# Four tiles' loads and transposes ahead of the weight pieces, and the second product of four tiles in step with w2

## The chip, the cores and the metric

The kernel runs on one core of a Trainium2 chip. The time is the device time of one execution in microseconds (us); a median of several runs is given, and beside it one execution taken with a profiler.

## The reference

The kernel computes banded attention with a per-head distance bias, followed by a normalised two-layer network with a residual. There are 4 batches, 8 heads, 768 tokens and a head size of 64; the model width is 512 and the inner width 2048. The weights arrive as 8-byte floats.

```
keep   = (col < n_global) | (0 <= row - col < n_local)       # 8 and 96
scores = q @ k.T / 8 - slope[h] * dist ; scores[~keep] = -1e9
a      = softmax(scores)
x      = (a @ v), heads side by side                          # [4, 768, 512]
xn     = (x - mean) / sqrt(var + 1e-6) * g_ln
out    = x + relu(xn @ w_ch1) @ w_ch2                         # [512,2048], [2048,512]
```

## The kernel before

**Tiles.** The 3072 tokens are cut into 24 tiles of 128 (`TILES`): first the four tiles at the head of each batch, which see only themselves (tiles 0 to 3, one key block), then the other twenty, which see their own block and the one before (two key blocks). Two tiles are a chunk (`CT = 2`), and the network works on a chunk of 256 tokens.

**A tile's way.** `keys` loads k, splits each value into two halves of 16 bits (`kn`, high and low part) and transposes them by DMA into `kT`; `attention` does the same with q (`qn`, `qT`, plus two DMAs, line 199, that lay a copy with the halves exchanged), and `values` with v, without a transpose. Then come the scores on TensorE (line 225), the mask and minimum on VectorE (230), the exponential on ScalarE (234), the split of the result (237 or 239, and 240 on GpSimd), a transposing DMA `pT<-pn` (242) and the product with v (250 to 252). `norm` ends the tile: statistics, scaling, a split, and a transposing DMA `xT<-xn` (273). A chunk's network waits for `xT` of both its tiles. All DMAs are issued from one queue, SyncE's (SP).

**The network.** `ffn1(c, f)` computes two blocks of 128 inner units for chunk c: 24 matmuls of 256 columns (lines 316 to 318), a ReLU (320) and a split (321) into a tile `h` of the pool `hpool` (17 buffers of 2 KB a partition). A chunk has eight such groups. `ffn2(c, n_)` computes the second product for one tile: 48 matmuls of 512 columns (331 to 333) into one bank of PSUM, then the residual (337) and the store (339).

**The weights.** They come in 16 pieces of 1 MB, eight of w1 (`weights1(j, c)`) and eight of w2 (`weights2(f)`). A piece is loaded into one of three buffers `st` (line 139), and then takes three passes on ScalarE (142, 144, 147) and three on VectorE (143, 145, 148) to become two matrices of 16-bit floats. Two pieces of w1 serve two groups of `ffn1`; a piece of w2 serves two of the sixteen steps of `ffn2`.

**The order.** The program is traced in Python; a scheduler then fixes each engine's order, in which what was traced earlier goes first among what its own model takes to be ready. Each engine and SP's queue then work in that fixed order. `ORDER` adds constraints: `mk` names instructions, and an entry such as `"D1_0_1": "q0"` puts the load of that piece behind tile 0's q transpose on SP's queue, if that was traced before. The start is traced so:

```
one = tokens(0); four steps of it; build_masks()
weights1(0, 0); weights1(0, 1)
go(both(one, tokens(1)))          # tiles 0 and 1
go(f1w(0, range(NK)))             # w1's other pieces, ffn1 of chunk 0 between them
go(tokens(2)); go(tokens(3))      # tiles 2 and 3
build_mask1(); four pieces of w2; ffn1 of chunk 1, w2's other pieces between
run(ffn2 of tiles 0 to 3, side(tiles 4 to 6), RATE)
```

After that `run` takes each chunk in turn, with the attention of later tiles between its steps (`side`). PSUM has four pools of two banks: `ps_s`, `ps_v`, `ps_1` (first product) and `ps_2` (second product).

## Time and profile before

| | us |
|---|---|
| median of 3 runs | 696.86 |
| lowest and highest | 696.26, 701.62 |
| profiled execution, its own time | 697.23 |
| its span | 695.5 |
| mean granted clock of TensorE | 0.982 of full speed |
| PE busy | 590.6 |
| VectorE (DVE) busy | 391.3 |
| ScalarE (ACT) busy | 293.6 |
| GpSimd (POOL) busy | 153.0 |

The span is the time from the profile's first instruction to its last; 1.7 us of the execution's own time lie outside it. Busy times are sums over the span, and the engines work beside each other. PE is TensorE's matmuls. [...]

### The profile page before, as it was taken

The numbers are of one execution on the slowest core, as the hardware profiler recorded it, in microseconds if no ns is written. First come the engines' busy times: TensorE is split into PE (matmuls) and PEld (weight loads), VectorE is DVE, ScalarE is ACT, GpSimd is POOL, SyncE is SP. The second block draws the span as 40 slices with busy tenths as digits, with TensorE's granted clock in tenths as the row PEclk, the third lists the DMA queues.
The fourth block names the chain that finished last, engine by engine and source line by source line (L and its number), as shares of the span: only waits on it lengthen the run. The fifth ranks groups of instructions, "written<-read, shape, count | busy, mean of one in ns | idle before, by whom it ended". The sixth has DMA issues, their size and how long they took to land. (4 is left out here: it accounts for less than half of the span.)

```text
span 695.5 us, 13443 instructions
## 1 busy us (share of the span) xinstructions
PE 590.6 (85%) x5218; PEld 417.0 (60%) x5218; DVE 391.3 (56%) x976; ACT 293.6 (42%) x752; POOL 153.0 (22%) x141
## 2 busy tenths in 40 slices
PE   1011499999589989989999999799989999999995
PEld 0011376785367577577596596396576586684762
DVE  4889899643657687466366456365445456342111
ACT  4977888423424342344354254253243254140110
POOL 0111213302312312222231322222231232120000
PEclk9999999999789999999999999999999999999998
DMA  9999999717867676766848646866853855231001
GB/s 212 245 295 281 243 290 207 161 21 126 167 113 152 127 153 107 149 124 138 158 96 150 146 97 133 148 108 122 167 116 69 152 89 92 66 62 31 16 1 36
DMA packets 264728, 93.25 MB, mean 134 GB/s; under 512 B 254416, under 2 KB 254416, under 8 KB 264656
## 3 DMA queue, kind: packets, MB, share of 16 engines
q1 hardware_dynamic: 264656, 92.31, 64.6%
q8 instruction: 43, 0.70, 0.4%
q14 instruction: 29, 0.24, 0.1%
HBM read 37.23 MB, written 6.29 MB: 63 GB/s over the span
## 5 line engine op out<-in xcount | busy, mean ns | idle before, releaser
L316 PE MATMUL f<-xT,w1h 128*128 128x256 f16 x768 | 212.1, 276 | 12.6 <-DMA xT<-xn 7.6
L317 PE MATMUL f<-xT,w1h 128*128 128x256 f16 x768 | 212.2, 276 | 0.0
L318 PE MATMUL f<-xT,w1l 128*128 128x256 f16 x768 | 212.1, 276 | 0.0
L240 POOL TENSOR_TENSOR pn<-T,pn 128x512 f16<-128x512 f32 x88 | 105.8, 1203 | 207.9 <-DVE pn L239 103.8
L331 PE MATMUL f<-w2h,h 128*128 128x512 f16 x384 | 146.3, 381 | 0.0
L332 PE MATMUL f<-w2l,h 128*128 128x512 f16 x384 | 146.2, 381 | 0.0
L333 PE MATMUL f<-w2h,h 128*128 128x512 f16 x384 | 145.7, 380 | 0.0
L320 ACT ACTIVATE h<-f 128x512 f16<-128x512 f32 x96 | 56.6, 592 | 128.6 <-PE f L318 128.5
L321 DVE SCALAR_TENSOR_TENSOR h<-f,h 128x512 f16<-128x512 f32 x96 | 65.7, 685 | 69.7 <-ACT h L320 69.5
L225 PE MATMUL s<-kT,qT 128*128 128x128 f16 x704 | 57.1, 230 | 51.4 <-DMA qT<-qn 25.3
L234 ACT ACTIVATE T<-T,mn 128x256 f32<-128x256 f32 (+1 forms) x192 | 92.3, 482 | 3.8
L317 PEld LDWEIGHTS <-w1h 128*128 128x128 f16 x768 | 76.0, 99 | 25.0 <-issue 13.7
L225 PEld LDWEIGHTS <-qT 128*128 128x128 f16 x704 | 48.3, 103 | 61.9 <-DMA qT<-qn 33.8
L316 PEld LDWEIGHTS <-w1h 128*128 128x128 f16 x768 | 76.2, 99 | 11.1 <-issue 0.2
L318 PEld LDWEIGHTS <-w1l 128*128 128x128 f16 x768 | 76.2, 99 | 9.5
L230 DVE CUSTOM_DVE_ANT_0 T<-s,mask 128x256 f32<-128x256 f32 (+1 forms) x192 | 67.2, 396 | 24.3 <-PE s L225 24.0
L250 PE MATMUL pv<-vn,pT 128*128 128x64 f16 x352 | 40.9, 196 | 33.3 <-DMA pT<-pn 33.2
L239 DVE CAST pn<-T 128x512 f16<-128x512 f32 x80 | 40.3, 504 | 46.5 <-ACT T L234 41.7
L333 PEld LDWEIGHTS <-h 128*128 128x128 f16 x384 | 37.8, 98 | 42.1 <-issue 0.8
L332 PEld LDWEIGHTS <-h 128*128 128x128 f16 x384 | 37.7, 98 | 39.4 <-issue 0.5
L331 PEld LDWEIGHTS <-h 128*128 128x128 f16 x384 | 37.7, 98 | 37.7 <-issue 0.6
L250 PEld LDWEIGHTS <-pT 128*128 128x128 f16 x352 | 32.7, 99 | 40.7 <-DMA pT<-pn 37.5
(91 smaller groups left out, 646.5 us busy)
## 6 DMA issues: line engine op xcount, KB each, us to landing
st<-in_moe_w_ch_dram SPq DMA_DIRECT2D x16, 1024.0 KB, 6.2
vf<-in_v_dram SPq DMA_DIRECT2D x27, 256.0 KB, 3.5
kf<-in_k_dram SPq DMA_DIRECT2D x26, 256.0 KB, 3.8
qf<-in_q_dram SPq DMA_DIRECT2D x24, 256.0 KB, 3.3
out_dram<-x SPq DMA_DIRECT2D x24, 256.0 KB, 2.4
qT<-qT SPq DMA_DIRECT2D x46, 128.0 KB, 2.5
pT<-pn SPq DMA_TRANSPOSE x88, 3.2
kT<-kn SPq DMA_TRANSPOSE x27, 3.9
```

The costliest lines, as they stand in the source:

```text
L225: last = chain(last, pe.matmul(ps[:, u, n_ * P:(n_ + 1) * P], lhsT=qT[:, a * H + h, :], rhs=use[n_][0][:, h, :], start=(a == 0), stop=(a = ...
L230: vec.tensor_tensor_reduce(out=T[:, u, :], in0=ps[:, u], in1=mask, scale=1.0 / Z, scalar=3e38, op0=ALU.add, op1=ALU.min, accum_out=nm[:, h ...
L234: mk(f"e{t}_{g}", act.activation(out=T[:, u, :], in_=T[:, u, :], func=AF.Exp, scale=-1.0, bias=mn[:, h:h + 1], accum_out=sm[:, h:h + 1]))
L240: pool.tensor_tensor(out=pn[:, :, 1, :], in0=T, in1=pn[:, :, 0, :], op=ALU.subtract)
L250: last = chain(last, pe.matmul(pv[:, h, :], lhsT=ph, rhs=vv[:, h, :D], start=(n_ == 0), stop=False))
L316: last = chain(last, pe.matmul(ps[:, a], lhsT=w1h[:, kk, fs], rhs=xT[:, kk, :], start=(kk == 0), stop=False))
L317: last = chain(last, pe.matmul(ps[:, a], lhsT=w1h[:, kk, fs], rhs=xT[:, NK + kk, :], start=False, stop=False))
L318: last = chain(last, pe.matmul(ps[:, a], lhsT=w1l[:, kk, fs], rhs=xT[:, kk, :], start=False, stop=(kk == NK - 1)))
L321: mk(f"l{c}_{f}", vec.scalar_tensor_tensor(out=hh[:, 1], in0=ps, scalar=0.0, in1=hh[:, 0], op0=ALU.max, op1=ALU.subtract))
L331: pe.matmul(ps, lhsT=hh[:, 0, tok], rhs=w2h[:, f, :], start=(f == 0), stop=False)
L332: pe.matmul(ps, lhsT=hh[:, 0, tok], rhs=w2l[:, f, :], start=False, stop=False)
L333: pe.matmul(ps, lhsT=hh[:, 1, tok], rhs=w2h[:, f, :], start=False, stop=(f == NF - 1))
```

## The change

Tiles 0 to 3 are traced first, in steps that are dealt out by hand: tile 0's k and q, tile 1's loads, the masks, tile 1's k and q, tile 2's loads, and so on to the loads and the k and q transposes of tile 3. Tiles 0 and 1 are then finished; tiles 2 and 3 run beside `f1w`, in which all eight pieces of w1 now stand (pieces (0,0) and (0,1) too). `ffn1` of chunk 1 follows whole, and after it `ffn2_first`: for each piece of w2, the two steps of the second product that it serves, for all four tiles, into four banks (two of `ps_2`, two of `ps_1`); beside it run tiles 4 to 6.

The loaded and split k, q and v of tiles 1 to 3, `kT` and `vn` of tiles 0 and 1, `qT` of tiles 2 and 3 and the output x of tile 5 lie in buffers of `hpool`. `qT` is two tiles in place of one. The loads of g_ln move behind the loads of tile 0. `ORDER` now holds ten entries beside the sixteen of the line below it. The amount of arithmetic, of weight passes and of transfers is the same.

```
...
 TILES = [(b, 0) for b in reversed(range(B))] + [(b, i) for b in range(B) for i in range(1, NT)]
-ORDER = {"D1_0_1": "q0"}
+ORDER = {"L2": "q0", "L3": "q1", "D1_0_0": "q0", "D1_0_1": "q1", "D1_1_0": "q1", "D1_1_1": "p1_0", "D1_2_0": "q3", "D1_2_1": "p2_0", "L4": "p3_1", "L5": "x3"}
 ORDER.update({f"X{n}": f"l{2 + n // 8}_{2 * n % 16}" for n in range(16)})
...
         if ORDER.get(key) in marks:
             tc.add_manual_dep(ins.ins, marks[ORDER[key]].ins.name, NOSYNC, reason="order")
+    place = {bi: t for t, bi in enumerate(TILES)}
+    def short(b, i, shape, dtype, tag, name, bufs):
+        if 0 < place[b, i] < 2 * CT and not (b, i) in again:
+            return hpool.tile(shape, dtype, tag="h", name=name)
+        return p2.tile(shape, dtype, tag=tag, name=name, bufs=bufs)
+    again = set()
+    def own(b, i, name):
+        if place[b, i] < CT and not (b, i) in again:
+            return hpool.tile([P, H, P], F16, tag="h", name=f"{name}{b}_{i}")
+        return p2.tile([P, H, P], F16, tag=name if i else name + "0", name=f"{name}{b}_{i}", bufs=3 if i else 2)
     def fetch(src, name, b, i):
-        f = p2.tile([P, H, D], F32, tag="ld", name=f"{name}f{b}_{i}", bufs=6)
-        load.dma_start(out=f, in_=src[b, :, i * P:(i + 1) * P, :].rearrange("h p d -> p h d"))
+        f = short(b, i, [P, H, D], F32, "ld", f"{name}f{b}_{i}", 6)
+        mk(f"L{place[b, i]}", load.dma_start(out=f, in_=src[b, :, i * P:(i + 1) * P, :].rearrange("h p d -> p h d")))
         return f
-    early = {name: fetch(src, name, *TILES[0]) for name, src in (("k", k), ("q", q))}
+    early = {}
+    def loads(t, names):
+        for name in names:
+            early[name, t] = fetch({"k": k, "q": q, "v": v}[name], name, *TILES[t])
+    loads(0, "kq")
+    def piece(src, name):
+        st = p3.tile([P, 2, 512], I64, tag="st", name="st" + name, bufs=3)
+        mk("D" + name, load.dma_start(out=st, in_=src))
+        return st
+    def piece1(j, c):
+        return piece(w1[2 * c * P:2 * (c + 1) * P, j * 512:(j + 1) * 512].rearrange("(a p) n -> p a n", a=2), f"1_{j}_{c}")
     cnt = counts(tc, const, load, n_global, n_local)
     ng, nl = cnt[:, 0:1], cnt[:, 1:2]
+    loads(0, "v")
...
     def keys(b, i):
-        kf = early["k"] if (b, i) == TILES[0] else fetch(k, "k", b, i)
-        kn = p2.tile([P, H, P], F16, tag="ld", name=f"kn{b}_{i}", bufs=6)
+        kf = early.pop(("k", place[b, i]), None) or fetch(k, "k", b, i)
+        kn = short(b, i, [P, H, P], F16, "ld", f"kn{b}_{i}", 6)
         act.activation(out=kn[:, :, :D], in_=kf, func=AF.Copy)
         (pool if i else vec).tensor_tensor(out=kn[:, :, D:], in0=kf, in1=kn[:, :, :D], op=ALU.subtract)
-        kT = p2.tile([P, H, P], F16, tag="kT" if i else "kT0", name=f"kT{b}_{i}", bufs=3 if i else 2)
-        sp.dma_start_transpose(out=kT, in_=kn.rearrange("p h d -> p (h d)"))
+        kT = own(b, i, "kT")
+        mk(f"k{place[b, i]}", sp.dma_start_transpose(out=kT, in_=kn.rearrange("p h d -> p (h d)")))
         return kT
     def values(b, i):
-        vf = fetch(v, "v", b, i)
-        vn = p2.tile([P, H, P], F16, tag="vn" if i else "vn0", name=f"vn{b}_{i}", bufs=3 if i else 2)
+        vf = early.pop(("v", place[b, i]), None) or fetch(v, "v", b, i)
+        vn = own(b, i, "vn")
         act.activation(out=vn[:, :, :D], in_=vf, func=AF.Copy, scale=VS)
         vec.scalar_tensor_tensor(out=vn[:, :, D:], in0=vf, scalar=VS, in1=vn[:, :, :D], op0=ALU.mult, op1=ALU.subtract)
         return vn
...
     def attention(t, x, xT, at):
         b, i = TILES[t]
         if i == 1 and b:
+            again.add((b, 0))
             blocks[b, 0] = keys(b, 0), values(b, 0)
             yield
         kT = keys(b, i)
-        qf = early["q"] if t == 0 else fetch(q, "q", b, i)
+        qf = early.pop(("q", t), None) or fetch(q, "q", b, i)
         yield
-        qn = p2.tile([P, H, P], F16, tag="ld", name=f"qn{t}", bufs=6)
+        qn = short(b, i, [P, H, P], F16, "ld", f"qn{t}", 6)
         act.activation(out=qn[:, :, :D], in_=qf, func=AF.Copy, scale=-QS)
         vec.scalar_tensor_tensor(out=qn[:, :, D:], in0=qf, scalar=-QS, in1=qn[:, :, :D], op0=ALU.mult, op1=ALU.subtract)
-        qT = p2.tile([P, 2 * H, P], F16, name="qT")
-        mk(f"q{t}", sp.dma_start_transpose(out=qT[:, :H, :], in_=qn.rearrange("p h d -> p (h d)")))
+        if CT <= t < 2 * CT:
+            qT = [hpool.tile([P, H, P], F16, tag="h", name=f"qT{t}_{a}") for a in range(2)]
+        else:
+            qT = p2.tile([P, 2 * H, P], F16, name="qT")
+            qT = [qT[:, :H, :], qT[:, H:, :]]
+        mk(f"q{t}", sp.dma_start_transpose(out=qT[0], in_=qn.rearrange("p h d -> p (h d)")))
         yield
         for here, there in ((slice(0, D), slice(D, P)), (slice(D, P), slice(0, D))):
             if t == 0:
-                vec.tensor_copy(out=qT[here, H:, :], in_=qT[there, :H, :])
+                vec.tensor_copy(out=qT[1][here], in_=qT[0][there])
             else:
-                load.dma_start(out=qT[here, H:, :], in_=qT[there, :H, :])
+                load.dma_start(out=qT[1][here], in_=qT[0][there])
         yield
         vn = values(b, i)
         blocks[b, i] = kT, vn
...
         c, at = divmod(t, CT)
         if at == 0:
             xTs[c] = p3.tile([P, 2 * NK, CT * P], F16, tag="xT", name=f"xT{c}", bufs=2)
-        xs[t] = xpool.tile([P, H, D], F32, tag="x", name=f"x{t}")
+        xs[t] = hpool.tile([P, H, D], F32, tag="h", name=f"x{t}") if t == 2 * CT + 1 else xpool.tile([P, H, D], F32, tag="x", name=f"x{t}")
         yield from attention(t, xs[t], xTs[c], at)
+    gs = const.tile([P, NK], F32, name="gs")
+    load.dma_start(out=gs, in_=g_ln.rearrange("(c p) -> p c", p=P))
+    gb = const.tile([P, DM], F32, name="gb")
+    load.dma_start(out=gb, in_=g_ln.partition_broadcast(P))
     masks = {}
     def build_masks():
...
         for a in range(2):
             hs[c, f + a] = hh[:, :, a, :]
-    def ffn2(c, n_):
-        t = c * CT + n_
-        tok = slice(n_ * P, (n_ + 1) * P)
-        ps = ps_2.tile([P, DM], F32, tag="f2", name=f"f2_{t}")
-        for f in range(NF):
-            hh = hs[c, f]
-            pe.matmul(ps, lhsT=hh[:, 0, tok], rhs=w2h[:, f, :], start=(f == 0), stop=False)
-            pe.matmul(ps, lhsT=hh[:, 0, tok], rhs=w2l[:, f, :], start=False, stop=False)
-            pe.matmul(ps, lhsT=hh[:, 1, tok], rhs=w2h[:, f, :], start=False, stop=(f == NF - 1))
-            if f % 4 == 3 and f < NF - 1:
-                yield
+    def product2(ps, t, f):
+        c, at = divmod(t, CT)
+        tok = slice(at * P, (at + 1) * P)
+        hh = hs[c, f]
+        return [pe.matmul(ps, lhsT=hh[:, a, tok], rhs=w, start=(f == 0 and n_ == 0), stop=(f == NF - 1 and n_ == 2))
+                for n_, (a, w) in enumerate(((0, w2h[:, f, :]), (0, w2l[:, f, :]), (1, w2h[:, f, :])))]
+    def result(ps, t):
         xx = xs[t].rearrange("p h d -> p (h d)")
         vec.scalar_tensor_tensor(out=xx, in0=ps, scalar=1.0 / (HS * WS), in1=xx, op0=ALU.mult, op1=ALU.add)
         b, i = TILES[t]
         load.dma_start(out=out[b, i * P:(i + 1) * P, :], in_=xx)
+    def ffn2(c, n_):
+        t = c * CT + n_
+        ps = ps_2.tile([P, DM], F32, tag="f2", name=f"f2_{t}")
+        for f in range(NF):
+            product2(ps, t, f)
+            if f % 4 == 3 and f < NF - 1:
+                yield
+        result(ps, t)
+        yield
+    def ffn2_first():
+        ps = [ps_2.tile([P, DM], F32, tag="f2", name=f"f2_{t}") if t < 2 else ps_1.tile([P, DM], F32, tag="f1", name=f"f2_{t}") for t in range(2 * CT)]
+        for f in range(0, NF, 2):
+            weights2(f // 2)
+            for t in range(2 * CT):
+                product2(ps[t], t, f)
+                product2(ps[t], t, f + 1)
+                yield
+        for t in range(2 * CT):
+            result(ps[t], t)
         yield
     def ffn(c):
...
     def f1w(c, js):
         for j in js:
             for c_ in range(NK // 2):
-                if j:
-                    weights1(j, c_)
+                weights1(j, c_)
                 yield
             for f in range(4 * j, 4 * j + 4, 2):
                 ffn1(c, f)
...
         for _ in g:
             pass
-    one = tokens(0)
-    for _ in range(4):
-        next(one)
+    first = [tokens(t) for t in range(2 * CT)]
+    def step(t, n):
+        for _ in range(n):
+            next(first[t])
+    step(0, 2)
+    loads(1, "kqv")
+    step(0, 2)
     build_masks()
-    weights1(0, 0)
-    weights1(0, 1)
-    go(both(one, tokens(1)))
-    go(f1w(0, range(NK)))
-    go(tokens(2))
-    go(tokens(3))
+    step(1, 2)
+    loads(2, "kqv")
+    step(0, 2)
+    step(1, 2)
+    step(2, 2)
+    loads(3, "kqv")
+    step(3, 2)
+    go(both(*first[:CT]))
+    run(f1w(0, range(NK)), both(*first[CT:]), 2.5)
     build_mask1()
-    for f in range(NF // 4):
-        weights2(f)
-    for f in range(0, NF // 2, 2):
+    for f in range(0, NF, 2):
         ffn1(1, f)
-    for f in range(NF // 4, NF // 2):
-        ffn1(1, 2 * f)
-        weights2(f)
     ahead = 2 * CT
     def side(to):
...
             yield from itertools.islice(g, 3)
         yield from g
-    run(seq(*(ffn2(c, n_) for c in range(2) for n_ in range(CT))), side(3 * CT + AHEAD), RATE)
+    run(ffn2_first(), side(3 * CT + AHEAD), RATE)
     for c in range(2, NC):
         g = side((c + 2) * CT + AHEAD)
         run(ffn(c), extremes(g) if c == 3 else g, RATE)
```

## Rows read from the trace of the kernel before

**Rows 1.** The page, busy tenths of PE and of the DMA engines in 40 slices.
```profile
PE   1011499999589989989999999799989999999995
...
DMA  9999999717867676766848646866853855231001
```

**Rows 2.** The windows by stage: busy us and instructions of each engine, granted clock, DMA share.
```profile
core 0: us, PE busy (x) PEld busy (x) DVE busy (x) ACT busy (x) POOL busy (x), PEclk, DMA share, GB/s
0.00:79.00 79.00, 9.69 (x99) 7.61 (x100) 61.48 (x137) 59.84 (x126) 13.29 (x18) 1.00 1.05 256
79.00:122.00 43.00, 40.17 (x336) 29.13 (x336) 39.09 (x62) 34.84 (x63) 8.77 (x6) 1.00 1.08 247
122.00:172.00 50.00, 49.70 (x434) 34.60 (x433) 25.05 (x72) 17.18 (x52) 12.38 (x11) 1.00 0.54 102
172.00:188.00 16.00, 9.07 (x80) 5.75 (x78) 9.77 (x30) 7.88 (x25) 4.45 (x4) 0.80 0.72 146
188.00:200.00 12.00, 9.54 (x83) 7.46 (x83) 3.73 (x7) 1.23 (x2) 2.30 (x2) 0.70 1.06 189
200.00:650.00 450.00, 434.51 (x3941) 307.86 (x3939) 245.45 (x658) 168.44 (x478) 111.76 (x100) 0.99 0.60 116
650.00:695.50 45.50, 37.97 (x255) 24.59 (x253) 6.77 (x14) 4.18 (x7) 0.00 (x0) 0.94 0.04 14
```

**Rows 3.** The timeline of PE, idle time before an instruction in brackets.
```profile
72.18 0.39 PE L225 MATMUL s<-kT,qT 128*128 128x128 f16 x2 [10.00 <-DMA qT<-qn]
78.99 0.37 PE L316 MATMUL f<-xT,w1h 128*128 128x256 f16 x1 [6.42 <-DMA xT<-xn]
...
180.88 1.72 PE L225 MATMUL s<-kT,qT 128*128 128x128 f16 x16 [3.53 <-DVE nm L230]
...
188.10 0.37 PE L316 MATMUL f<-xT,w1h 128*128 128x256 f16 x1 [0.92 <-DMA xT<-xn]
...
195.65 0.24 PE L250 MATMUL pv<-vn,pT 128*128 128x64 f16 x1 [2.36 <-DMA pT<-pn]
```

**Rows 4.** The timeline of SP's queue, transposes of tiles 0 and 1.
```profile
48.65 1.25 SPq L273 DMA_TRANSPOSE xT<-xn  x1
...
75.29 1.27 SPq L273 DMA_TRANSPOSE xT<-xn  x1
```

**Rows 5.** The DMA of the first 80 us: GB/s by slice, issues with times to landing.
```profile
GB/s 5 233 86 148 380 207 244 265 362 374 311 60 297 266 239 245 213 194 336 278 239 426 393 291 190 231 170 352 278 181 201 412 265 327 292 173 399 263 220 183
...
st<-in_moe_w_ch_dram SPq DMA_DIRECT2D x12, 1024.0 KB, 6.2
...
kT<-kn SPq DMA_TRANSPOSE x5, 6.3
```

**Rows 6.** The groups by line of 0 to 220 us, passes of VectorE over a piece.
```profile
L143 DVE SCALAR_TENSOR_TENSOR st<-st 128x1024 int32<-128x1024 int32 x16 | 20.5, 1281 | 8.2 <-ACT st L142 8.1
...
L145 DVE SCALAR_TENSOR_TENSOR st<-st 128x1024 int32<-128x1024 int32 x16 | 19.4, 1214 | 2.9 <-ACT st L144 2.9
```

**Rows 7.** The line L148, ns min/median/max, first and last start.
```profile
L148 DVE TENSOR_TENSOR w1l<-st,w1h x8: 1204/1211/1751, 20.9 to 64.5; 128x1024 f16<-128x1024 f32 x8
L148 DVE TENSOR_TENSOR w2l<-st,w2h x8: 1206/1225/2183, 76.0 to 120.2; 128x1024 f16<-128x1024 f32 x8
```

**Rows 8.** The timeline of PE, neighbouring matmuls of the two products.
```profile
79.16 0.42 PE L317 MATMUL f<-xT,w1h 128*128 128x256 f16 x1
79.37 0.42 PE L318 MATMUL f<-xT,w1l 128*128 128x256 f16 x1
...
88.56 0.27 PE L316 MATMUL f<-xT,w1h 128*128 128x256 f16 x1
88.67 0.27 PE L317 MATMUL f<-xT,w1h 128*128 128x256 f16 x1
...
166.18 0.38 PE L331 MATMUL f<-w2h,h 128*128 128x512 f16 x1
166.40 0.38 PE L332 MATMUL f<-w2l,h 128*128 128x512 f16 x1
```

14 lines of the change are left out of this document (4 added, 10 removed).

## The prediction, made before the change was run

> **What bounds the kernel now.** I read the slices of the page first, to see where TensorE is idle at all [rows 1]: its first five slices are nearly empty, then it is full but for one slice at about 174 to 191 us. The windows by stage turn that into microseconds [rows 2]. In the first 79 us PE works 9.7, so 69.3 are idle. From 79 to 172 it works 89.9 of 93. From 172 to 188 it works 9.1 of 16 at a granted clock of 0.80, from 188 to 200 it works 9.5 of 12 at 0.70. From 200 to 650 it works 434.5 of 450: there PE is the bound, and the change touches nothing in it. The last 45.5 us hold 38 of work. So what can be won lies ahead of 200 us: the start, and the dent from 172 to 200.
>
> The timeline of PE says what ends the two [rows 3]. The start ends at 78.99, when `xT<-xn` of tile 1 lands; until then chunk 0 has nothing to multiply. The dent is a chain of scores that wait for VectorE, then chunk 2's first product waiting for its `xT` until 188.10, then 2.4 us of waiting for `pT` at 195.65.
>
> What holds tile 1 up to 79? SP's queue issues tile 0's `xT` at 48.65 and tile 1's only at 75.29 [rows 4]. Beside them VectorE is busy 61.5 of 79 us and the DMA engines read 1.05 of their capacity, 1.08 in the next 43 us [rows 2]. In that time 12 pieces of the weights have been issued (the twelfth at the very end) and all five `kT` transposes up to tile 4 [rows 5]; the eight pieces of w1 are through by 65.7 and then lie unused until 79 [rows 7]. So the weights come too early and the activations too late, on DMA engines and vector passes that are both nearly full.
>
> **The change, part by part.** The sum is made against the profiled execution, 697.2 us (span 695.5 and 1.7 around it), which is 0.4 above the median of 696.9. A measurement of this kernel tells about 1% from no change, so 7 us.
>
> *The start.* I call T the time at which chunk 0's first product begins. The 12 loads and 8 transposes of k and q of the four tiles go ahead, but tiles 0 to 3 had them inside the first 79 us before as well [rows 5]; they are no new work ahead of T. What leaves that stretch is weight pieces: `ORDER` lets two in by the q transposes, a third and fourth behind `q1` and `p1_0`, and with three buffers I count 4 handled or under way by T, where 11.5 had come before. Removed: 7.5 pieces. The price of a piece on the DMA engines lies between 1.05 MB at the fastest slice of that stretch, 426 GB/s, or 2.5 us, and 1.05 MB at its mean of 256 GB/s, or 4.1 [rows 2, 5]; I take 3, nearer the fast end, as a piece has long rows. That is 22.5 us, and T = 79 − 22.5 = 56.5. Bounds: with 4.1 us it would be 48; and tile 0, which met the same contention, had its activations issued at 48.65 [rows 4], so 47 is about the floor. If tiles 2 and 3 get between tile 1 and its passes on VectorE (six passes of q, k and v, some 0.7 to 1.6 us each, and the queue places of four transposes), or only 4 pieces really leave, T is 66.
>
> A `kT` transpose takes 6.3 us from issue to landing in this stretch, queueing included [rows 5]; the trace has no row for its own share of the engines, so the sum does without it. [...]
>
> *The queue.* On SP's queue the new order entries are constraints of place, not waits: `D1_1_1` stands behind `p1_0`, `L4` behind `p3_1`, `L5` behind `x3`. But each transposing DMA waits on the queue for its data, and whatever stands behind it waits too: pieces behind `p1_0`, tile 4 behind tile 3's `pT`. I cost `L4` and `L5` at nothing because tile 3 is done some 20 us after T and tiles 4 and 5 are needed only at the end of the second product, about 100 us after T; without that cover each late microsecond would show at chunk 2.
>
> *The first product of chunk 0.* It now runs in step with w1. Two neighbouring matmuls of it start 0.11 us apart [rows 8], so 192 of them are 21 us in four blocks of 5.2. Pieces come every 6.2 us: eight of w1 end between 20.9 and 64.5, eight of w2 between 76.0 and 120.2 [rows 7]; the two passes of lines 143 and 145 and that of line 148 alone are 1.28 + 1.21 + 1.2 = 3.7 us of VectorE for each [rows 6, 7], so this is no idle pace. With four pieces ready at T, blocks 0 and 1 run at once, the last piece of w1 is there at T + 4 × 6.2 = T + 24.8, and its block ends at T + 30. Added stall: 9 us. With two ready it is 21.5, with six it is none. Tiles 2 and 3's scores and products with v lie in these waits.
>
> *The rest up to chunk 2.* Chunk 1's first product (21 us) needs no new piece. Then the second product takes 24 matmuls, 0.22 us apart [rows 8], for each piece: 5.2 us, and with tiles 4 to 6 among them about 6.7. w2's pieces follow at 6.2 from T + 24.8, so three are ready when it begins at T + 51, and the last is there at T + 74, needed at T + 98. No stall as long as a piece takes under some 8 us. Between 79 and 188 PE did 98.9 us of work, which is this same set of products and tiles within 1 us (tile 6's product with v in, half of tile 7's scores out), some 2 of it inflated by the low clock of the dent [rows 2]; I take 97. Four banks of PSUM are held until the end of the second product, so chunk 2 waits for at least one residual pass; with pauses of the in-order queue for `pT` or scores I add 5 us, and bound that by nothing and by 15 (the whole idle time of 200 to 650).
>
> Tile 5's x in `hpool` is the seventeenth buffer beside sixteen `h`; tile 6's x must wait for a stored output of tiles 0 to 3. I cost both at nothing: chunk 3 needs tile 6 only a chunk (about 50 us) later. Moving the two loads of g_ln and splitting `qT` cost nothing either; the first stand behind loads that tile 0 needs anyway.
>
> *The sum.* Chunk 2 begins at 56.5 + 97 + 9 + 5 = 167.5, where it began at 188.1: 20.6 us sooner. From 188 to 200 the kernel before also lost 2.4 us of idle time and, at 0.70 of the clock, some 3 more; with tiles 4 to 6 traced early in a longer second product I take 4 of these back. 697.2 − 20.6 − 4 = 672.6.
>
> **The rivals.**
>
> *Everything is fed.* T = 47, six pieces ready, stalls of 3 and 3: chunk 2 at 150, 38 sooner, and 5 regained: 654. For it: the DMA engines at 1.08 with a piece at 2.5 us leave room; against it: VectorE's 100 us of work up to 122 [rows 2], which the change doesn't shorten.
>
> *Bursts at the low clock.* Behind its 6.4 us of idle time the first product began with matmuls 0.21 us apart, 1.2 GHz for 256 columns, against 0.11 later [rows 3, 8]. If all four blocks of chunk 0 run so between their waits, its 192 matmuls take 41 us for 21; 9 of the 20 more lie in the stall already counted, so 11 are added: 683. [...]
>
> *The order moves little.* The scheduler may fill idle places with pieces as before, T stays at 79, and only the smoother second product shows: 7 us of idle time from 172 to 188 and 4 behind it, so 686.
>
> *Nothing to gain at the DMA engines.* They are full up to 122 us [rows 2], and all transfers remain. If T is 66, three pieces are ready (stall 15) and tiles 4 to 6 fight with w2 for the queue (stall 10), chunk 2 begins at 188 as before, and only the dent's end is regained: 693.
>
> *Slower: the weights become the end.* If the tiles keep VectorE and the queue so busy that no piece is through at T = 66, all sixteen follow; at 8 us each, because tiles 2 to 6 share the engines now, the last is there at 194, its 5 us of product end at 199, and chunk 2 begins 11 later than before: about 704, with 4 regained. It decides once 66 + (16 − n) × 8 + 5 passes 188, at one ready piece or none; at 7 us a piece it does not. Against it: VectorE is idle 17.5 of the first 79 us even now [rows 2], and a piece needs 3.7 there.
>
> **How the numbers follow.** The forecast gets 0.50 and by itself runs from 664 to 683 (T 4 us to either side, stalls 5 shorter to 6 longer); everything fed 0.15; low clock 0.08; the order moves little 0.08; DMA-bound 0.12; slower 0.07. Faster by over 1% (below 690) are the first four, 0.81; within 1% the fifth, 0.12; slower 0.07. The range goes from 657 to 692: it leaves out about half of the fed case, half of the DMA case and the slow one, together near 0.2.
>
> **What would show it.** In the profile after: chunk 0's first product begins near 56 us, with at most six pieces handled before; four blocks of it with gaps that end on passes of w1; a first product of chunk 1 without gaps; no `w2` wait in the second product; chunk 2's first matmul near 168; and everything behind it as before, shifted. The prediction is wrong if tile 1's `xT` is still late (then the wait ahead of it names what replaced the weights), if TensorE waits for `w2l` or `w2h` in the second product, or if the dent returns because chunk 2's `xT` is late again.

## The result, and the profile after

The changed kernel takes 690.9 us (median of 7 runs, 687.6 to 693.6) beside 697.2 for the kernel before in the same runs (7, 694.2 to 701.6): a ratio of 0.9897 with a 95% interval of 0.9857 to 0.9936. In a later comparison, with 5 runs of it and 21 of before, it was 0.9909 [0.9881, 0.9937]. So the change gains 1%, some 6 us, where 24 were forecast. The profiled execution took 689.44 us, 16.8 above the forecast.

I use three times for every kernel: T, when chunk 0's first product begins; C1, when chunk 1's begins; C2, when chunk 2's begins. C1 and C2 are the 193rd and the 385th matmul of the first product in the timeline of PE. That timeline of the kernel after:

```profile
61.55 0.37 PE L353 MATMUL f<-xT,w1h 128*128 128x256 f16 x1 [4.38 <-DMA xT<-xn]
...
104.70 0.27 PE L353 MATMUL f<-xT,w1h 128*128 128x256 f16 x1
...
135.04 0.37 PE L353 MATMUL f<-xT,w1h 128*128 128x256 f16 x1 [4.10 <-DVE h L358]
...
181.92 0.27 PE L353 MATMUL f<-xT,w1h 128*128 128x256 f16 x1
```

T came 17.4 us sooner (78.99 before, [rows 3]) and C2 only 6.2 (188.10 before). Behind C2 the span has 505.8 us left, where it had 507.4. So the start won 17.4, and 11.2 were given back between T and C2. In the execution profiled again T came at 63.3 and C2 at 181.7, so the same kernel gave back 9.2 there: the loss is known to about 2 us. The windows by stage of the kernel after, and then of before for the same piece of work (its T to its C2):

```profile
core 0: us, PE busy (x) PEld busy (x) DVE busy (x) ACT busy (x) POOL busy (x), PEclk, DMA share, GB/s
0.00:61.55 61.55, 11.47 (x112) 9.18 (x113) 40.19 (x129) 37.51 (x98) 10.76 (x16) 1.00 0.96 214
61.55:104.70 43.15, 32.70 (x265) 24.52 (x265) 36.50 (x51) 34.26 (x61) 12.77 (x6) 0.88 0.91 227
104.70:181.92 77.22, 70.65 (x580) 45.17 (x577) 59.93 (x124) 48.12 (x109) 22.95 (x18) 0.98 0.92 200
61.55:181.92 120.37, 103.35 (x841) 69.69 (x840) 96.43 (x174) 82.38 (x169) 35.71 (x24) 0.94 0.92 210
181.92:650.00 468.08, 449.28 (x4077) 319.11 (x4077) 249.59 (x666) 169.69 (x481) 113.16 (x101) 0.99 0.61 116
```

```profile
79.00:188.10 109.10, 98.94 (x846) 69.48 (x846) 73.90 (x162) 59.89 (x140) 25.60 (x21) 0.97 0.78 166
```

PE has nearly the same matmuls in the stretch (841 and 846), but takes 120.4 us for them instead of 109.1. VectorE has 96 us of work in it where it had 74, ScalarE 82 where it had 60: the passes over the pieces of w1 moved from before T to behind it. What PE waited for from T to C2 (the second row, `xT`, is the wait that ends at T; the last two rows are of the kernel before, from its T to its C2):

```profile
PE f L353 <- DVE h L358: 6.0, 5, 4.1
PE f L353 <- DMA xT<-xn: 4.4, 1, 4.4
PE pv L283 <- DMA pT<-pn: 4.3, 3, 2.4
PE f L353 <- ACT h L357: 3.1, 1, 3.1
PE f L353 <- ACT w1h L175: 1.5, 1, 1.5
PE f L366 <- ACT w2h L175: 0.7, 1, 0.7
PE f L355 <- DVE w1l L176: 0.6, 1, 0.6
PE f L366 <- DVE w2l L176: 0.6, 1, 0.6
...
PE f L316 <- DVE h L321: 1.7, 1, 1.7
PE pv L250 <- DMA pT<-pn: 1.1, 1, 1.1
```

Only 3.4 us (1.5 + 0.7 + 0.6 + 0.6) wait for a piece. 9.1 wait for a split of `h` (6.0 on its half by VectorE, 3.1 on that by ScalarE): the first product's result goes through one pass of ScalarE and one of VectorE before its PSUM bank is free. The longest of these is worth following back through the timelines of ScalarE, VectorE and SP's queue:

```profile
128.10 0.58 SPq L120 DMA_DIRECT2D vf<-in_v_dram  x1
...
131.48 0.63 ACT L205 ACTIVATE vn<-vf 128x512 f16<-128x512 f32 x1 [2.17 <-DMA vf<-in_v_dram]
132.02 1.11 ACT L175 ACTIVATE w2h<-st 128x1024 f16<-128x1024 f32 x1
133.04 0.57 ACT L357 ACTIVATE h<-f 128x512 f16<-128x512 f32 x1
...
134.31 0.68 DVE L358 SCALAR_TENSOR_TENSOR h<-f,h 128x512 f16<-128x512 f32 x1
```

The load of tile 6's v was issued at 128.10; ScalarE, whose order is fixed, waits 2.2 us for it; a pass over a piece of w2 stands next; only then comes `h`, and VectorE's half of it 1.3 us later. TensorE waits 4.1 us for work that neither of these loads feeds.

For the rest of the loss I priced the matmuls of the stretch by the distance of neighbours at a granted clock of 1.00 (0.109 us in the first product, as from 97.2 to 99.7 in the kernel after, 0.216 in the second, 0.056 for a score, 0.029 for a product with v), took the gaps in PE's timeline as idle time, and what is left as loss to the low clock. Every kernel below is broken up in the same way, so the parts can be compared, though each is good to about 1 us. The last column is too high by some 2 us, as it also holds the moments at the edges of gaps: the matmuls at double their distance (0.21 us in the first product, from 93.3 to 94.5 in the kernel after, where the granted clock is 0.50) cost 2.8 us in the kernel before and 7.0 in the kernel after, counted from the timelines. The difference between the kernels is nearly the same either way, 3.9 or 4.2.

| T to C2 | us | work | idle | low clock |
|---|---|---|---|---|
| before | 109.1 | 94.5 | 9.3 | 5.5 |
| after | 120.4 | 94.0 | 17.0 | 9.4 |

So of the 11.2 us given back 7.7 are more idle time and 3.9 the clock; the work is 0.5 less.

### The profile page after: what moved, and what is told of

It is laid out like the page before. It is cut to its first block, busy times and chain, and to the rows that moved or that the text cites. A ratio compares the mean times of both kernels' runs of the same rounds, so it can differ in the third digit from the quotient of the medians.

```text
span 687.7 us, 13440 instructions
## 1 busy us (share of the span) xinstructions
PE 594.5 (86%) x5218; PEld 416.2 (61%) x5218; DVE 391.4 (57%) x976; ACT 292.6 (43%) x752; POOL 159.6 (23%) x141
## 4 chain that ended last, share of the span: by engine, by line
PE 49%; DMA 23%; SPq 8%; DVE 6%; issue 5%; ACT 5%; POOL 3%; POOLq 0%; ACTq 0%; DVEq 0%
PE f L366 23%; DMA pT<-pn 7%; PE f L353 7%; PE f L355 7%; PE f L354 7%; DMA kf<-in_k_dram 6%; PE s L258 3%; DMA qT<-qn 3%; SPq L275 3%; DMA st<-in_moe_w_ch_dram 3%; SPq L232 2%; SPq L199 2%; ACT T L267 1%; POOL pn L273 1%; PE pv L283 1%
## 5 line engine op out<-in xcount | busy, mean ns | idle before, releaser
L366 PE MATMUL f<-w2h,h 128*128 128x512 f16 x768 | 237.5, 380 | 0.7 <-ACT w2h L175 0.7
L366 PEld LDWEIGHTS <-h 128*128 128x128 f16 x1152 | 109.9, 98 | 120.3 <-issue 3.8
L358 DVE SCALAR_TENSOR_TENSOR h<-f,h 128x512 f16<-128x512 f32 x96 | 65.7, 685 | 54.4 <-ACT h L357 54.3
L300 POOL TENSOR_TENSOR rs<-rs,half 128x1 f32<-128x1 f32 x24 | 26.8, 1118 | 138.2 <-DVE rs L299 138.2
L289 DVE TENSOR_TENSOR x<-pv,r 128x512 f32<-128x512 f32 x24 | 16.5, 689 | 68.1 <-PE pv L285 68.1
L197 POOL TENSOR_TENSOR kn<-kf,kn 128x512 f16<-128x512 f32 x20 | 25.7, 1283 | 125.6 <-ACT kn L196 125.6
```

Source lines behind the costliest of these rows:

```text
L358: mk(f"l{c}_{f}", vec.scalar_tensor_tensor(out=hh[:, 1], in0=ps, scalar=0.0, in1=hh[:, 0], op0=ALU.max, op1=ALU.subtract))
L366: return [pe.matmul(ps, lhsT=hh[:, a, tok], rhs=w, start=(f == 0 and n_ == 0), stop=(f == NF - 1 and n_ == 2)) for n_, (a, w) in enumerate ...
```

## The experiments

All edits are to the kernel after, but for the two that take one part of the change. "Rest" is what the span holds behind C2; the ratio is to the kernel before, with its 95% interval.

Two things limit what the table can say. First, almost every edit made the scheduler lay out the queues anew. In the whole program only "after, again" and f1 have the change's order on every engine and on SP's queue, and e7 has it but for 12 matmuls; in all others the order changed before C1 or soon after it, so none of them takes away one thing alone. Second, C1 does not stand behind the same work everywhere: of the second product's matmuls 12 come ahead of it in the kernel after, but 96 before, 24 in e1 and g1, 64 in e2, 36 in e6 and f3, 32 in e11. C2 stands behind the same first and second products in all.

| kernel | T | last of w1 | C1 | C2 | rest | ratio |
|---|---|---|---|---|---|---|
| before | 79.0 | 65.7 | 130.0 | 188.1 | 507.4 | |
| after | 61.6 | 95.6 | 104.7 | 181.9 | 505.8 | 0.990 [0.986, 0.994] |
| after, again | 63.3 | 96 | 105.4 | 181.7 | 506.6 | 0.991 [0.988, 0.994] |
| e3 start alone | 63.3 | 98 | 107.1 | 190.0 | 506.7 | 1.002 [1.000, 1.004] |
| e4 second product alone | 79.5 | 66 | 133.3 | 188.3 | 504.8 | 0.997 [0.995, 0.999] |
| e1 fourth piece earlier | 64.8 | 93 | 108.1 | 180.4 | 506.8 | 0.985 [0.981, 0.989] |
| e2 no entries for pieces | 72.7 | 79 | 116.8 | 185.8 | 506.2 | 0.995 [0.992, 0.998] |
| e12 less on VectorE | 69.5 | | 108.6 | 188.4 | 504.2 | 0.996 [0.993, 1.000] |
| e5 less on VectorE, zeroing first | 70.1 | | 109.4 | 188.5 | 502.4 | 0.998 [0.996, 1.001] |
| e6 half the bytes | 66.7 | 84 | 106.9 | 183.1 | 506.4 | 0.993 [0.990, 0.995] |
| e7 lower rate of side work | 63.0 | 95 | 104.3 | 180.9 | 504.8 | 0.990 [0.987, 0.993] |
| e8 filler matmuls | 63.7 | 94 | 108.6 | 181.7 | 511.3 | 0.997 [0.993, 1.001] |
| e9 two buffers | 60.4 | 103 | 111.4 | 189.1 | 505.8 | 0.995 [0.992, 0.997] |
| e10 half pieces | 60.4 | 94 | 104.4 | 180.7 | 510.7 | 0.993 [0.991, 0.996] |
| e11 = e10 with e1 | 63.7 | 90 | 107.8 | 181.4 | 514.0 | 0.993 [0.990, 0.996] |
| f1 tiles 2, 3 not needed | 62.4 | 94 | 102.6 | 181.1 | 509.4 | 0.991 [0.988, 0.994] |
| f2 = f1 on e11 | 64.1 | 91 | 104.0 | 179.1 | 510.1 | 0.991 [0.988, 0.994] |
| f3 = e1 with e7 | 64.2 | 86 | 110.3 | 181.6 | 507.9 | 0.996 [0.994, 0.998] |
| g1 tile 5 earlier | 62.5 | 96 | 109.8 | 185.6 | 504.6 | 0.994 [0.991, 0.996] |
| g2 tiles 2, 3 behind tile 1 | 61.7 | 90 | 100.8 | 179.6 | 506.8 | 0.987 [0.984, 0.989] |

T of the same kernel differs by 1.8 us between two profiled executions and C2 by 0.3, so C2 is the time to go by. In e8, e10, e11, f1 and f2 the rest is 4 to 8 us longer than after the change; I have not followed that, and judge them by C2. As f1 has the change's order to the end, 3.6 us of such a difference can come without any other order.

### The two halves of the change

e3 has the start of the change and the old second product, e4 the old start and the new second product:

```
e3: for f in range(NF // 4): weights2(f)  ...  run(seq(*(ffn2(c, n_) ...)), side(...), RATE)
e4: ORDER, loads and blocks as before;    run(ffn2_first(), side(3 * CT + AHEAD), RATE)
```

> The first part alone: four tiles ahead as changed, but the second product of tiles 0 to 3 tile by tile and the w2 pieces as in the kernel before. Theory A (the start gives 17 us at T and loses them to w1's late pieces, and what is left of the gain is the dent): T stays near 61.6, the dent ahead of chunk 2 comes back (idle time of 7 us or more behind 165), and the time is 693 to 698. Theory B (the gain that is left comes from the earlier T, the second product only costs): T near 61.6, no such dent, 684 to 690.

> The second part alone: start as in the kernel before (first product from 79 us), chunk 1's first product whole, then the second product of the four tiles in step with w2, tile 5's x in the pool of h. Theory A: the dent goes, chunk 2 begins some 5 to 9 us sooner than at 188, and the time is 688 to 692, much of what the whole change gives. Theory B: the second product waits for its four banks and its pieces, nothing is won, 695 to 700.

e3: T comes 15.7 us sooner and C2 1.9 later than before, 1.002 [1.000, 1.004]. The time, 700.9, lies above both expected ranges. The stretch is 126.7 us with 19.7 idle and 12.9 lost to the clock. Its waits (from T, whose own 4.3 is in the second row) are spread over tiles, weights and the dent's chain of scores:

```profile
PE pv L283 <- DMA pT<-pn: 7.6, 4, 3.8
PE f L353 <- DMA xT<-xn: 6.3, 2, 4.3
PE s L258 <- DVE nm L263: 4.0, 2, 2.2
PE f L366 <- ACT w2h L175: 3.3, 2, 2.5
```

The dent is back, as one of the expectations had it (the row `nm`). e4: C2 as before (+0.2), the rest 2.6 shorter, 0.997. Neither half gains half a per cent, both together 1%. The start alone only moves the idle time behind T; with the second product in step with w2's pieces some of it is kept.

### Does the order of the pieces hold the time?

e1 lets the fourth piece go at `q1` and drops the entry for the sixth; e2 drops all entries for pieces but the old one:

```
- ... "D1_0_0": "q0", "D1_0_1": "q1", "D1_1_0": "q1", "D1_1_1": "p1_0", "D1_2_0": "q3", "D1_2_1": "p2_0" ...
e1:
+ ... "D1_0_0": "q0", "D1_0_1": "q1", "D1_1_0": "q1", "D1_1_1": "q1", "D1_2_0": "q3" ...
e2:
+ ... "D1_0_1": "q0" ...
```

> The changed kernel with two order entries altered: the fourth piece of w1 stands behind q1 instead of p1_0, and the sixth has no entry (it stood behind p2_0). In the changed kernel the fourth and fifth piece are issued at 51.6 us, and VectorE and ScalarE both pause there (VectorE 46.7 to 51.9, ScalarE 44.9 to 54.9). Theory A (the entries hold pieces back while both engines that handle them idle): the fourth piece is handled in that pause, T stays within 2 us of 61.6, the last piece of w1 ends near 89 instead of 95.6, chunk 0's first product ends 6 to 7 sooner than 100.0, and the time falls by 5 to 7 us, to about 683 to 685. Theory B (the engines that handle pieces have no room that the tiles don't need): T goes up by 3 to 5 us as the piece gets between tile 1's passes, and the time is unchanged or up to 4 us longer, 689 to 694.

> The changed kernel with the order entries of all w1 pieces taken out but the one that the kernel before had (second piece behind q0). Six pieces now stand on SP's queue ahead of tile 1's xT, where the changed kernel has five with two of them late. Theory A: the last piece of w1 ends near 84 instead of 95.6, T moves up by at most 3 us, the time falls by 6 to 10 us, to 680 to 684. Theory B: T goes up toward the 79 of the kernel before (70 or more), and the time is 690 to 697.

e1: T is 3.2 us later, C2 1.5 sooner; its idle time is 14.0 and its loss to the clock 7.4. e2: T goes to 72.7, 11.2 later, for a C2 that is 3.9 later; its stretch is 113.1 with 11.9 and 6.8. Counted by the last pass over a piece, 3 pieces are through by T in the change, 4 in e1, 7 in e2 and 9 before, and T is 61.6, 64.8, 72.7 and 79.0: some 2.9 us for each, or 2.6 if the repeated run's 63.3 is taken for the change; the one piece of e1 is too little to tell. A piece let in ahead of T is paid there, and part of it comes back before C2: e2's T is 11.2 later and its stretch 7.3 shorter, e1's T 3.2 later and its stretch 4.7 shorter. The interval of e1's ratio overlaps with that of the change.

### One resource at a time

Four edits are meant to take away what each of four theories holds responsible: VectorE (its third pass over a piece is left out, so the low halves of the weights are zero, set once by GpSimd; in e5 ahead of everything, in e12 a little later), the DMA engines (only half of each piece is loaded, the other half is zeroed by GpSimd), the side work of tiles 2 and 3 between the blocks of chunk 0 (at a lower rate), and the low clock (96 matmuls into a bank that is not read).

```
e5, e12: - vec.tensor_tensor(out=dl, in0=u, in1=dh, op=ALU.subtract)
         + pool.memset(w1l, 0.0); pool.memset(w2l, 0.0)
e6: - load.dma_start(out=st, in_=src)
    + pool.memset(st[:, 1].bitcast(F32), 0.0); load.dma_start(out=st[:, 0], in_=src[:, 0])
e7: - run(f1w(0, range(NK)), both(*first[CT:]), 2.5)
    + run(f1w(0, range(NK)), both(*first[CT:]), 0.6)
e8: + for _ in range(12): pe.matmul(idle, lhsT=w1h[...], rhs=xTs[c][:, 0, :], start=True, stop=True)
```

> The changed kernel without the last VectorE pass of every weight piece (16 passes of 1.2 us, 20 us of VectorE); the low halves of w1 and w2 are zeroed once by GpSimd at the start, so the output lacks their part. Loads and ScalarE passes are all there. Between the first product's start (61.6) and chunk 2's (181.9) the changed kernel has 94.0 us of PE work, 17.0 idle and 9.4 lost to the low clock. Theory V (VectorE sets the pace of that stretch): it shortens by 10 us or more, 674 to 682. Theory D (the DMA engines, 0.92 busy in it, set the pace): by 3 us at most, 687 to 691. Theory Q (fixed queues, in which a late transfer holds up passes behind it, set it): 3 to 6 us, 684 to 688.

> The run with VectorE relieved of each piece's last pass, once more, with the zeroing on GpSimd behind the two small constants, which it had held up by 14 us in the earlier one (so that its T was 70.1). The low halves of the weights are zero, so the output lacks their part. Theory V (VectorE sets the pace): 20 us less of its work give 10 us or more, 674 to 681. Theory S: a piece stays about 2 us less in its buffer, the pace falls by some 0.6 us and w1 by 3: 684 to 688. Theory Q: 2 us at most, 687 to 692.

> The changed kernel with half the bytes of each weight piece: only the first half of its rows is loaded, the other half is zeroed by GpSimd, so the output lacks half the weights. All passes on VectorE and ScalarE stay. 8 of the 16.8 MB of weights leave the DMA engines, some 20 to 25 us of their time by the price of 2.5 to 3 us a piece. Theory D: the stretch from 61.6 to 181.9 shortens by 10 us or more, T falls by 2 to 4, 672 to 680. Theory V: 3 us at most, 686 to 691. Theory Q: transfers land earlier, so the passes behind them wait less: 4 to 8 us, 682 to 687.

> The changed kernel with tiles 2 and 3 dealt out at 0.6 instead of 2.5 steps per step of w1, so that w1's pieces come before most of their attention. Theory V (the tiles take VectorE and ScalarE from w1's pieces): w1's last piece ends near 86 instead of 95.6 and chunk 0's product near 92 instead of 100; chunk 1's then waits for tile 3, so of the 8 us 3 to 5 remain: 684 to 687. Theory Q: w1 ends sooner but chunk 1's product and tiles 4 and 5 come as much later, 688 to 694.

> The changed kernel with 12 added matmuls of 256 columns behind each of the eight groups of chunk 0's first product (10.5 us of PE in all at full clock), into a bank that nobody reads, so that PE is less idle between the bursts. In the changed kernel the bursts from 61.6 to 100 lose some 6 us to the low clock and have 9 us of idle time. Theory C (the low clock behind gaps costs what the slow matmuls show): those 6 us shrink to 3 or less, the added matmuls lie in idle time, 684 to 689. Rival: the gaps end on weights and splits anyway, so a faster burst only waits longer, and the added matmuls cost up to 5 us: 690 to 696.

e5 and e12 moved their own start: T went to 70.1 and 69.5. This is read from the timelines of GpSimd and VectorE in e12:

```profile
1.40 6.92 POOL L190 MEMSET w1l<- 128x8192 f16 x1
8.26 6.95 POOL L191 MEMSET w2l<- 128x8192 f16 x1
...
8.38 6.85 DVE L67 TENSOR_SCALAR neg<-nf 128x2 f32<-128x2 f32 x1
```

The same pass in the kernel after, without the zeroing:

```profile
6.82 0.17 DVE L67 TENSOR_SCALAR neg<-nf 128x2 f32<-128x2 f32 x1
```

A pass over two elements a partition took 6.85 us beside a zeroing of 6.95, and 0.17 without one; it began 0.12 us behind the zeroing's start and ended 0.02 behind its end. So the two kernels tell nothing by their time. From T on, the stretch of e12 is 118.9 us instead of 120.4, with VectorE busy 81.6 instead of 96.4: 15 us less of its work returned 1.5, and the repeated run of the change, which takes nothing away, has 118.3. No wait for a piece is left in e12 and those for `h` fall from 9.1 to 5.1 us, but its idle time is 17.0 as in the change: 4.2 us now wait for a copy into `kT` on VectorE, 1.8 for chunk 1's `xT`, and 6.1 for `pT`.

e6: the DMA share of the stretch falls from 0.92 to 0.75 and w1 is through at 84 instead of 96, but the stretch is 116.3 long (15.2 idle, 6.6 lost to the clock), 4.0 less. T is 5.1 later, with five pieces through by then instead of three: per piece that is nearly as much as in the other runs, though each has half the bytes. From T to C1 the idle time and the loss to the clock together are about 9 us instead of 17; C1 comes only 3 us nearer to T as 24 more matmuls of the second product stand ahead of it, and behind C1 the idle time grows. A split of `h` again makes PE wait 4.4 us, near 130:

```profile
PE f L354 <- DVE h L359: 8.0, 6, 4.4
PE pv L284 <- DMA pT<-pn: 6.5, 3, 3.5
```

e7: C2 1.0 sooner, the same time within the intervals. But the edit hardly reached the program: every queue has the change's order, except that TensorE does one block of 12 products with v behind 21 more matmuls of the first product, at 69.75 us instead of 66.81. So e7 is nearly a third execution of the change and says nothing about side work. e8: the loss to the clock falls to 2.5 and the idle time to 10.3, but 10.4 us of filler work stand in their place; the stretch is 2.4 shorter (2.1 for the repeated run without filler), C2 where it was and the kernel no faster. Its window shows the granted clock at 0.99 where it was 0.94:

```profile
63.70:181.65 117.95, 107.69 (x938) 77.82 (x937) 96.98 (x169) 81.84 (x169) 36.19 (x24) 0.99 0.95 214
```

### The buffers of the pieces

A piece occupies its buffer from the issue of its load to the end of its last pass, 13 to 22 us, most of them 17 to 22; with three buffers that is one piece in 6 to 7 us. In the kernel after the loads of the seventh to the twelfth piece were issued within 0.5 us of the moment in which a buffer came free. e9 has two buffers; e10 pieces of half the size in six; e11 is e10 with the entries of e1.

```
-      st = p3.tile([P, 2, 512], I64, tag="st", name="st" + name, bufs=3)
e9:  + st = p3.tile([P, 2, 512], I64, tag="st", name="st" + name, bufs=2)
e10: + st = p3.tile([P, 1, 512], I64, tag="st", name="st" + name, bufs=6)
```

> The changed kernel with two buffers for weight pieces instead of three. In the changed kernel a piece stays 17 to 22 us in its buffer, from the issue of its load to the end of its last pass, and from the seventh piece to the twelfth each load is issued within 0.5 us of the end of the piece three before. Theory S (the three buffers set the pace of the pieces, and the pieces hold the first products): pieces come every 9 to 10 us instead of 7, the last piece of w1 ends 12 us or more later, and the time rises by 12 to 30 us, 702 to 720. Theory Q (the fixed order of the queues, whatever the buffers): under 6 us, 688 to 697.

> The changed kernel with pieces of half the size, 512 KB, in six buffers of half the size (the same 24 KB): 32 loads and 192 passes of about 0.65 us for 16 and 96 of 1.2 us, order entries as they were, for both halves. Theory S: a buffer is free after some 14 us instead of 19, as landing and passes are shorter; 1 MB then takes 5 to 5.5 us instead of 7, w1 ends 6 to 10 us sooner than 95.6, and the time falls by 5 to 10 us, 681 to 686. Theory Q: the same waits on the same queues, and 96 more passes with their fixed cost: 689 to 696.

> Half pieces in six buffers, and the order entries of the run with the fourth piece earlier (fourth behind q1, sixth without entry). There T went up by 3.2 and the seventh to twelfth piece again were issued the moment a buffer came free. Theory S: 3 us or so better than half pieces alone, 678 to 683. Theory Q: as the half pieces or worse, 689 to 697.

e9: C1 is 6.7 us later, as w1's last piece is done at 103 and the stretch from T to C1 is 51.0 long with 17.2 idle. The longest wait in it, 7.6 us, ends at 101.24 on tile 4's copies of q, just before that piece's first half is there. C2 is 7.2 later, so hardly more, though w2's pieces now come every 8.4 us (107.9 to 167.0) instead of every 6.7 (100.7 to 147.5). The pace of w2 matters little up to there, and the 8 us that the prediction named as its limit was not too high. e10 and e11 bring w1 in at 94 and 90, but C1 comes at 104.4 and 107.8 all the same (in e11 with 20 more matmuls of the second product ahead of it, 4.3 us), and C2 at 180.7 and 181.4. Pieces that come sooner find PE waiting for something else.

### What holds chunk 1?

In f1 chunk 1's first product multiplies the activations of chunk 0 once more, so that it doesn't need tiles 2 and 3; f2 does this in e11. f3 joins the entries of e1 with the lower rate of e7; f4 is the change itself ("after, again" in the table).

```
f1, f2: - xT = xTs[c]
        + xT = xTs[0 if c == 1 else c]
```

> Chunk 1's first product multiplies chunk 0's activations a second time, so it need not wait for tiles 2 and 3 (their part of the output is then another one; the work is the same). Joint theory (tiles 2 and 3 and the last piece of w1 come at about the same time): chunk 1's first product begins near 101 us instead of 104.7, held by the last piece at 95.6 and the rest of chunk 0's product, and chunk 2's moves by 4 us at most, 178 to 182. Rival (the activations of tiles 2 and 3 alone hold it): chunk 2's begins 8 us or more sooner, 174 or less, and the kernel takes some 681 us.

> The same on the kernel with half pieces and the earlier fourth piece, where w1 was through at about 90 us and chunk 1's first product still began at 107.8 us. Joint theory: with both constraints gone it begins at 93 to 98 us, and chunk 2's at 168 to 174 instead of 181.4. Rival (the time goes to the in-order queues whatever chunk 1 waits for): chunk 1's begins there too, but the gain is given back again before chunk 2's, which begins at 178 or later.

> The earlier fourth piece and the slower side work of tiles 2 and 3 together. If the two small gains (chunk 2's first product 1.5 and 1.0 us sooner) add up, it begins at 179.4 us and the kernel takes 2 to 4 us less than the change; if both shift the same waits, 180.4 and no less than the better of the two alone, within 1 us of the change in the median.

> The changed kernel itself, as the yardstick for the three others on the same chip: 0.985 to 0.994 of the kernel before, chunk 2's first product at 182 us.

f1: C1 at 102.6, C2 at 181.1, 2.8 and 0.5 sooner than its yardstick, with every queue in the same order. So chunk 1's need of their activations alone doesn't hold it, as the joint theory said. f2: C1 comes at 104.0, not at 93 to 98, and C2 at 179.1: the joint theory fails there, and of the rival only the late C2 came. But f1 and f2 take away the need and not the place: the products of tiles 2 and 3 with v still stand in TensorE's order among the groups of chunk 0, and it waits there for their `pT`. Two rows of f1, and below them one of f2:

```profile
76.18 0.20 PE L283 MATMUL pv<-vn,pT 128*128 128x64 f16 x1 [1.88 <-DMA pT<-pn]
82.05 0.20 PE L283 MATMUL pv<-vn,pT 128*128 128x64 f16 x1 [1.70 <-DMA pT<-pn]
...
75.19 0.23 PE L287 MATMUL pv<-vn,pT 128*128 128x64 f16 x1 [3.46 <-DMA pT<-pn]
```

So what tiles 2 and 3 cost by their place is not tested. From T to C1 39.9 us remain in f2, 27.6 of work, 7.6 idle and 4.8 lost to the clock. Its waits up to C2:

```profile
PE pv L287 <- DMA pT<-pn: 9.7, 5, 3.5
...
PE f L357 <- DVE h L362: 3.6, 3, 2.0
```

f3: C2 as the change's (181.6), and 0.996 against 0.991 for the change beside it, which neither expectation had. The two small gains don't add up; that of e7, by its order, was none.

### The longest wait, and T itself

g1 lets the loads of tile 5, and with them tile 6's, go earlier; g2 writes the steps of tiles 2 and 3 behind those of tile 1:

```
g1: - "L5": "x3"
    + "L5": "p3_1"
g2: - step(1, 2); loads(2, "kqv"); step(0, 2); step(1, 2); step(2, 2); loads(3, "kqv"); step(3, 2)
    - go(both(*first[:CT]))
    + step(1, 2); step(0, 2); step(1, 2); go(both(*first[:CT]))
    + loads(2, "kqv"); step(2, 2); loads(3, "kqv"); step(3, 2)
    - "L2": "q0", "L3": "q1"
    + "L2": "q1", "L3": "p1_0"
```

> The loads of tile 5, and tile 6's behind them, may go behind tile 3's second pT instead of behind its x. Theory (each wait behind T counts at its length): the 4.1 us that TensorE waits at 135 us for a split of h, behind ScalarE's wait for tile 6's v, are gone and chunk 2's first product comes 4 us sooner, near 178. Rival (VectorE, ScalarE and the queue hand the time on): the wait is gone or moved, others of the same kind appear, and chunk 2's stays at 181 to 183.

> The steps of tiles 2 and 3 (loads, transposes, passes of q, k and v) are written behind those of tile 1, not between them. Theory (these steps on the in-order queues are why chunk 0's first product began 5 us later than forecast): it begins at 55 to 58 us instead of 61.6 to 63.3. Tiles 2 and 3 come as much later, so chunk 1's first product does not come sooner and chunk 2's stays at 180 to 184. Rival (the chain of tile 1 itself, its norm on GpSimd among it, sets the time): chunk 0's begins at 60 us or later as before.

g1: the wait of 4.1 us at 135 is 2.1, but others of its kind keep the sum at 6.7, the loss to the clock is 13.1, and C2 is at 185.6, later than the rival's 181 to 183, behind a residual pass:

```profile
PE f L353 <- DVE h L358: 6.7, 7, 2.1
...
PE f L353 <- DVE x L371: 3.3, 1, 3.3
```

So halving the longest wait, with the queues laid out anew, made C2 3.7 us later. Waits behind T don't count at their length.

g2: the steps moved, and T did not: 61.7. Tile 1's scores are multiplied at 25.80 us instead of 33.96, eight us sooner, but the second half of them passes VectorE at 41.66 where it did at 40.52. The timelines of g2, and below of the kernel after (PE's scores, VectorE's masks):

```profile
25.80 1.65 PE L258 MATMUL s<-kT,qT 128*128 128x128 f16 x14 [4.44 <-DMA qT<-qT]
...
27.33 0.28 DVE L263 CUSTOM_DVE_ANT_0 T<-s,mask 128x128 f32<-128x128 f32 x1
...
41.66 0.27 DVE L263 CUSTOM_DVE_ANT_0 T<-s,mask 128x128 f32<-128x128 f32 x1
```

```profile
33.96 1.65 PE L258 MATMUL s<-kT,qT 128*128 128x128 f16 x14 [1.35 <-DMA qT<-qT]
...
35.37 0.28 DVE L263 CUSTOM_DVE_ANT_0 T<-s,mask 128x128 f32<-128x128 f32 x1
...
40.52 0.28 DVE L263 CUSTOM_DVE_ANT_0 T<-s,mask 128x128 f32<-128x128 f32 x1
```

In the change tile 1's scores come late, because its copies of q stand on SP's queue behind tile 2's transpose of k, and between the halves VectorE has tile 0's norm, tile 2's k and one pass over a piece. In g2 they come early, and seven passes over pieces stand there, 8.9 us by their rows. What tile 1 gains on the queue it loses in that order, and a fourth piece is through by T (its last pass begins at 50.70), where the change has three. At 2.9 us a piece that could mean that the steps of tiles 2 and 3 cost about as much as a piece, and that what they left free went to a piece and not to T; it is not shown, as T of the same kernel differs by 1.8, and as many pieces are issued by T in g2 as in the change, five. g2 is at 0.987 [0.984, 0.989], its C2 at 179.6 with 13.9 us idle. That is the lowest C2 of all runs but f2, which does another product, but its interval overlaps with the change's, as e1's does: no version is shown to beat the change.

## Why the prediction was right or wrong

*What bounds the kernel: right.* Everything behind C2 stayed, 505.8 us against 507.4, and T is where time was won.

*The direction: right, and little more.* The forecast lay at 672.6; 690.9 lies just inside the range, but above the forecast's own 664 to 683, and by the prediction's own classes (below 690, or within 1%) in the one that got 0.12. That fewer pieces ahead of T bring T forward holds; what the stretch behind T loses, and why a piece costs what it does ahead of it, were wrong. The 16.8 us that the profiled execution is above the forecast divide into three terms of the sum: 5.0, 9.4 and 2.4.

*T, "79 − 22.5 = 56.5": 61.6, so 5 too early.* The price in it, 3 us a piece, came out (2.6 to 2.9 by the change). The step that failed is the count, "Removed: 7.5 pieces". By the prediction's own measure, pieces issued, five had been issued by T and not four, of 11.5: 6.5 at 3 us would give 59.5. By the last pass, 9 were through before and 3 after, and 79 − 6 × 3 is 61. The second fits the change, e1 and e2 better; in g2, with four through and five issued, T is the change's, which speaks for the first. The runs don't settle which of the two T answers to. That the price came out was luck in part: I had taken it from the DMA engines' rate, near its fast end for a piece's long rows, an estimate that no run tests; in e6, with half the bytes a piece, five pieces through go with a T of 66.7, on the same line, and g2 shows time paid elsewhere, by passes over pieces between tile 1's two halves on VectorE, where a piece has 3.7 us. That tiles 2 and 3 get "between tile 1 and its passes on VectorE", the prediction's reason for a T of 66, is not shown to cost anything: with them behind tile 1 T was the same (g2).

*The stalls, "9" and "5", with 97 of work, 111 in all: 26.4 us of idle time and low clock with 94 of work, 120.4, so 9.4 too few.* This is the largest miss, in the step on the first product of chunk 0. Of its 9 us of waits for pieces 3.4 came, though three pieces were ready and not four, and the last of w1 came at T + 34 instead of T + 24.8; with w1's end 12 us sooner (e6) the stretch to C2 is 4 us shorter, or 2 against the repeated run. What the step put at nothing is the splits of `h`: 9.1 us of waits, where before had 1.7 (7.6 in the repeated run). The forecast also took the low clock out of its work and put nothing in its place, and the table has 9.4 for it, of which 7.0 show in the distances of the matmuls. The 5 us for `pT`, scores and residuals were near: 4.3 for `pT` (6.8 in the repeated run). In the rows followed above the splits stand behind passes over pieces, now behind T, in the same in-order queues of ScalarE and VectorE. "A first product of chunk 1 without gaps" was wrong for the same reason: its gap at 135 is 4.1 us.

*The rival "bursts at the low clock"* got 0.08 and a price of 11; 3.9 us more than before were lost that way, a part of the miss. Its 1.2 GHz is 256 columns in 0.21 us, worked out and not recorded: the trace's records of the granted clock begin at 82.6, at 1.00, where the double distance ends (in the kernel after at 66.3), and the windows print 1.00 for the time ahead of them. From 188 to 190 the same distance goes with a recorded 0.50. In e8, with filler in the gaps, the granted clock was 0.99 instead of 0.94 and the loss 2.5 us instead of 9.4, and no time was gained.

*What is regained behind C2, "4": 1.6.*

*Right at their size:* no stall at w2's pieces as long as one takes under some 8 us (1.3 us of waits; e9); the work, 94 us for 97. (Three pieces of w2 were to be ready at "T + 51"; by the prediction's own pace it is four, which changes nothing.) An earlier tile 5 returned nothing that `L5` costs (g1). The rivals "everything fed" and "the weights become the end" did not come; "the order moves little" and "nothing to gain at the DMA engines" come near in time (686, 693), but T did move, and halving the bytes won 4 us of the stretch, not more.

*What stays open.* No relief (VectorE 1.5 us of the stretch, bytes 4.0, the clock 2.4, the need of tiles 2 and 3 2 to 3 us at C1) returns the 11.2, and the repeated run is 2.1 shorter without any. As these edits but f1 also laid out the queues anew, they bound what each resource is worth and don't isolate it. That the loss lies in the fixed order in which the passes stand on ScalarE and VectorE is argued from the waits and from e12, g1 and g2, where other waits took the place of one that had gone; a kernel that keeps every other queue and changes only the order of these passes was not tried, and neither was one that takes tiles 2 and 3 out of TensorE's order ahead of C1.

## What to carry to other kernels

Work that is moved from before an engine's start to behind it isn't gone: count its passes in the queues of the engines behind that point, together with the passes by which the busy engine gets its buffers back. A stall summed from one producer ("a piece each 6.2 us") is a floor; where ScalarE and VectorE are busy for 68% and 80% of the stretch and keep their order, as here, the loss was about twice the stall that I had summed. Count moved work at one point of its way, the same in both kernels. Two halves of a change can each be worth next to nothing alone. And where a scheduler lays out the queues, compare their order before and after an edit: e7 changed almost nothing, and most other edits changed more than they name.
